# Tiles 2 and 3 join the seven-product scheme in a layer-normed attention and MLP kernel on one core

## The chip, the cores and the metric

The kernel runs on one core of a Trainium2 chip. The time is device microseconds of one launch, as the median of 3 runs. The core has TensorE (PE in the profile; its weight loads are PEld), VectorE (DVE), ScalarE (ACT), GpSimd (POOL) and SyncE (SP), which here only issues transfers. ScalarE issues some transfers too, and waits in its own order to do so.

## The reference, cut to what matters

```python
x = A_x                                    # [1, 2048, 512], float32
xn = layernorm(x)                          # over the last axis, no scale or shift
q, k, v = split(xn @ wqkv)                 # 32 heads of 16
logits = q . k[pos - 2*w], w = 0..7        # times 16 ** -0.5; -1e9 where pos - 2*w < 0
s = (softmax(logits) . v[pos - 2*w]) @ wo
h = relu(xn @ w1 + b1) ** 2                # w1: 512 x 1792
g = silu(h @ w2 + b2)                      # w2: 1792 x 512
out = x + s * g
```

All of it is float32. A product of two float32 matrices is made from three passes: each operand is split into a rounded high part (written by ScalarE) and a low part (the rest, a subtraction on VectorE or GpSimd), and high by high, high by low and low by high are added up in one accumulator.

## The kernel before, in words

The 2048 rows are 16 tiles of 128. The kernel has two stages. In the first, each tile is loaded (`load_x`, line 146), its mean and spread are found (`stats`, `mean`, `spread`), it is normalised (`norm`, line 442), turned so that the 512 columns lie on partitions (`trans`, line 474) and split (`highx`, `lowx`). Tiles 0 to 3 are turned by TensorE (`TURN` is 4). Later tiles are turned in two steps: `shuffle` (line 467) moves blocks by four transfers on SP's queue (`xb<-xn`), and VectorE's stream transpose does the rest. Then q, k and v are formed and stored to DRAM; attention reads them back from there. In the second stage the MLP runs in four chunks of four tiles, and the attention's result meets it through `wo`.

Products of the first stage are made in two ways. The plain way, `qkv(t, s)` (line 526), takes 12 matmuls of 128x512 for one tile and one of q, k, v. The other way, `seven(a)` (line 571), treats a pair of tiles a and a+1 and the q and k columns as a 2 by 2 block product and forms it from seven block products instead of eight, with sums of blocks on both sides. The names: X, Y, Z and U are accumulators; `ss` holds the sums of the pair's turned tiles (four blocks in two buffers: `sum_x` makes the difference `xd` on VectorE and three more sums on GpSimd, `sum_high` and `sum_low` split them, one low part on VectorE and one on GpSimd); T1 to T4 (`t` in the profile) hold the sums of the weight blocks, made once by `sum_w` (line 556): eight subtractions, eight high parts, eight low parts. In the seven way, k's two output tiles are finished by additions on VectorE (`stg<-Z,stg`, `stg<-Y,stg`), while the plain way evacuates each output with one ScalarE copy. v is plain in both ways. Six matmuls make one block product. The last product of a pair, Z with T4, waits in `tail` and is issued in the next pair's turn.

Before the change `SEVEN` is the even tiles 4 to 14: tiles 0 to 3 are plain, and six pairs use seven products.

The order of the instructions on every engine is that of the program's text (`Ordered`, line 75, records each operation, so that all of them have line 87 in the profile). Attention is a generator of pieces of VectorE work of about 2.3 us. `pump(margin)` (line 366) keeps two estimated clocks, one for TensorE and one for VectorE, and lays down pieces as long as VectorE's estimated clock stays below TensorE's plus the margin. Loads of attention's k, q and v (`load`, line 322) are put off to a due time on those clocks and issued on ScalarE's queue.

Of the kernel before, what the change touches and what calls it, by code (L numbers as in the profile page):

```python
# [39 lines left out]

SEVEN = range(4, 15, 2)

# [5 lines left out]
ASIDE = (1, 3, 6, 9, 12)  # L48

STATS = (0, 1, 2, 3, 4, 5, 8, 10, 12)  # L50

MATMUL, TRANSPOSE, DVE_FIXED, SLACK, LATE, ROOM0, ROOM = 227, 150, 170, 500, 3000, 500, 3500

BEHIND, FREE, LAND, LOAD = 5000, 2000, 6000, 11500


@with_exitstack
def body(ctx: ExitStack, tc: tile.TileContext, x, wqkv, wo, w1, b1, w2, b2, out):
# [78 lines left out]
    pss = p1ctx.enter_context(tc.tile_pool(name="pss", bufs=1))  # L137
    G.memset(pxT.tile([P, 24], F32, name="gap"), 0.0)
    xins = {}
# [99 lines left out]
    def attention():  # L239
# [94 lines left out]

# [107 lines left out]
    def norm(t):  # L442
# [31 lines left out]
    def trans(t, aside=False):  # L474
        place(t)
        pTs[t] = piece(f"xs{t}") if t % 2 and t - 1 in SEVEN else psT(f"pxT{t}")
        if t < TURN:
# [19 lines left out]

    sums, ss = {}, {}

    def sum_x(a):  # L500

        xe, t = pTs.pop(a), pTs.pop(a + 1)
        u = piece(f"xd{a}")
        V.tensor_sub(u, xe, t)
# [9 lines left out]

    def sum_high(a):
        ss[a] = [pss.tile([P, 2, 2, 2, P], FR, name=f"ss{a}_{i}", tag="ss", bufs=2) for i in range(2)]
        for t, d in zip(sums[a], ss[a]):
            A.activation(d[:, :, 0], four(t), AF.Copy)

# [35 lines left out]

    def sum_w():
        q, k = raws[0], [raws[1, i] for i in range(KT)]
        for i in range(2):
            V.tensor_sub(q[:, i], k[i], q[:, i])
            V.tensor_sub(k[i], k[2 + i], k[i])  # L560
            V.tensor_sub(k[2 + i], k[2 + i], q[:, i])
            V.tensor_sub(q[:, 2 + i], q[:, 2 + i], k[2 + i])
        for n, src in ((T2, k[2:]), (T1, [q[:, 0], q[:, 1]]), (T3, k[:2]), (T4, [q[:, 2], q[:, 3]])):
            tw[n] = buffer(f"t{n}", n)
            for i in range(2):
                high(tw[n][:, 0, i], None, src[i])
                low(tw[n][:, 0, i], tw[n][:, 1, i], src[i], V)

    tail = []

    def seven(a):
# [28 lines left out]
        if a == SEVEN[0]:  # L600
            sum_high(a)
        first_norm(a)
        second_norm(a)
        pump(LATE)
        qkv(a, 2)
        if a > SEVEN[0]:
            sum_high(a)
        pump(LATE)
        while tail:
            tail.pop()()  # L610
        sum_low(a)
        if more:
            trans(a + 2)
        else:
            load_w(3)
        pump(LATE)
        qkv(b, 2)
        if more:
            trans(b + 2, True)
            lowx(a + 2)  # L620
# [7 lines left out]
        if more:  # L628
            highx(b + 2)
        else:  # L630
# [4 lines left out]
        if more:  # L635
            lowx(b + 2)
            sum_x(a + 2)
            next_stats(a)
        pump(LATE)
        product(Z, s(2), tw[T3])  # L640
        product(Y, s(3), wq[3], stop=True)
        pump(1500)
        V.tensor_add(sk_[:, :, 1], groups(Z), sk_[:, :, 0])
        V.tensor_add(sk_[:, :, 0], groups(Y), sk_[:, :, 0])
        store(a, 1, sk_)
# [7 lines left out]
        if not more:  # L653
# [3 lines left out]
            up(0, 0, psT)  # L657
            tail.pop()()
            next_w()
            pump(1500)  # L660
            up(0, 1, psT)
            lowh(0)
            pump(LATE)
# [88 lines left out]
    qkv(1, 0, lambda: highs(2, 2))  # L752
    trans(3)
    lows(2, 2)
    lowx(3)
    stats(4)
    stats(5)
    next(stream)
# [12 lines left out]
    def first_norm(a):  # L771
        if a + 4 < NT:
            norm(a + 4)

    def second_norm(a):
        if a + 4 < NT:
            norm(a + 5)
# [7 lines left out]

    for a in range(2, NT, 2):
        b = a + 1
        if a >= TPC:
            for t in (a, b):
                dma(sx[t // TPC][:, t % TPC], xt[t].bitcast(F32))  # L790
        if a in SEVEN:
            seven(a)
            if a + 2 < NT:
                pump(LATE)
            if a == 12:
                next_w()
                dma(b1t, b1.rearrange("(f p) -> p f", p=P))
            if a == 10:
                for f in range(3):
                    load_w(f)  # L800
            continue
        qkv(a, 0)
        pump(LATE)
        qkv(b, 0)
        if a == 2:
            first_norm(2)
            second_norm(2)
        trans(a + 2)
        pump(LATE)
        qkv(a, 1)  # L810
        lowx(a + 2)
        trans(b + 2)
        pump(LATE)
        qkv(b, 1)
        lowx(b + 2)
        sum_x(a + 2)
        pump(LATE)
        qkv(a, 2)
        next_stats(a)
        pump(LATE)  # L820
        qkv(b, 2)
        pump(LATE)
    lowh(1)
# [197 lines left out]
```

## Time and profile before

| what | value |
|---|---|
| median of 3 runs | 486.58 us (486.3 to 486.68) |
| the profiled execution, whole | 487.03 us |
| its span, first to last instruction | 485.0 us |
| granted TensorE clock | 0.998 |
| TensorE busy | 478.9 us, 99% of the span |
| VectorE busy | 439.8 us, 91% |
| ScalarE, GpSimd busy | 228.2 us (47%), 173.7 us (36%) |

In the timeline a row gives the start and the length in us, the engine, the line, the operation, what is written from what, the shape and the count, and in brackets how long the engine stood idle just before and what released it. The length of a row of several instructions runs to the end of the last. Neighbouring instructions of one engine overlap a little, so that the step from one start to the next is shorter than the length: matmuls of 128x512 show 389 ns each and follow each other every 227 ns.

### The profile page before, as it was taken

What the parts mean: (1) busy time and instruction counts of PE and PEld (TensorE: products, weight loads), DVE (VectorE), ACT (ScalarE), POOL (GpSimd) and SP (SyncE); (2) the same over time, 40 slices, a digit from 0 to 9 for tenths busy, and PEclk for the clock granted to TensorE, in tenths of its full rate; (3) what the DMA queues carried; (4) which work ended last, traced back from release to release, by engine and by line L of the source; (5) the groups of instructions that cost most, each with busy time, mean ns of one, the idle gap of its engine ahead of it and who ended that gap; (6) DMA issues with size and microseconds to landing.
All of it is one profiled execution on the core that took longest, in us unless ns stands there. A gap on an engine that the chain in (4) does not pass through costs nothing.

```text
span 485.0 us, 5918 instructions
## 1 busy us (share of the span) xinstructions
PE 478.9 (99%) x2118; PEld 394.4 (81%) x2118; DVE 439.8 (91%) x374; ACT 228.2 (47%) x403; POOL 173.7 (36%) x153
## 2 busy tenths in 40 slices
PE   8999999999999999999999999999999999999996
PEld 5888888888788888887888888888888888888885
DVE  5998999999999999999999999999999889999242
ACT  5686667635465774337313533461243365223240
POOL 1326343655798898201233230412032014021100
PEclk9999999999999999999999999999999999999999
DMA  8899898994969782805362428355421846150231
GB/s 280 245 309 314 251 277 282 316 344 174 320 225 298 180 268 92 298 34 190 104 187 64 164 96 283 100 151 166 128 100 67 297 101 170 37 151 0 88 105 68
DMA packets 48520, 88.78 MB, mean 183 GB/s; under 512 B 5372, under 2 KB 32364, under 8 KB 45676
## 3 DMA queue, kind: packets, MB, share of 16 engines
q1 hardware_dynamic: 42444, 51.72, 34.3%
q10 hardware_dynamic: 4320, 33.56, 19.4%
q0 software_dynamic: 1728, 3.15, 4.0%
q8 instruction: 16, 0.26, 0.2%
q14 instruction: 12, 0.10, 0.1%
HBM read 57.94 MB, written 27.32 MB: 176 GB/s over the span
## 4 chain that ended last, share of the span: by engine, by line
PE 98%; DMA 1%; DVE 0%; POOL 0%; issue 0%; ACT 0%; POOLq 0%
PE ph L87 31%; PE pb L87 31%; PE pq L87 14%; PE pw L87 9%; PE Z L87 3%; PE Y L87 3%; PE X L87 3%; PE U L87 2%; DMA x<-in_A_x 1%; PE pxT L87 0%; DVE z L87 0%; DVE st L87 0%; POOL rs L87 0%; DVE xn L87 0%; ACT scratch L87 0%
## 5 line engine op out<-in xcount | busy, mean ns | idle before, releaser
L87 PE MATMUL pb<-w,h 128*128 128x512 f32 x672 | 160.6, 389 | 0.0
L87 PEld LDWEIGHTS pb<-w,h 128*128 128x128 f32 x672 | 126.2, 188 | 26.2
L87 PE MATMUL ph<-xU,w 128*128 128x512 f32 x504 | 120.7, 389 | 0.0
L87 PEld LDWEIGHTS ph<-xU,w 128*128 128x128 f32 x504 | 94.5, 188 | 20.0 <-DVE h L87 0.5
L87 ACT ACTIVATE ph<-ph,b1t 128x512 f32<-128x512 f32 x56 | 36.9, 659 | 145.2 <-PE ph L87 131.6
L87 DVE TENSOR_TENSOR pv<-v,L 128x2048 f32<-128x2048 f32 x32 | 77.8, 2431 | 1.3 <-POOL L L87 0.7
L87 DVE TENSOR_TENSOR pr<-k,q 128x2048 f32<-128x2048 f32 x32 | 78.3, 2447 | 0.6
L87 DVE TENSOR_REDUCE L<-pr 128x128 f32<-128x2048 f32 x32 | 72.9, 2279 | 0.4
L87 DVE TENSOR_REDUCE v<-pv 128x256 f32<-128x2048 f32 x32 | 72.7, 2272 | 0.4
L87 POOL TENSOR_TENSOR h<-sq,h 128x512 fp32r<-128x512 f32 x15 | 25.9, 1729 | 82.1 <-ACT sq L87 79.7
L87 PE MATMUL pw<-wot,oT 128*128 128x512 f32 (+1 forms) x204 | 45.9, 376 | 0.0
L87 DVE TENSOR_TENSOR h<-ph,h 128x512 fp32r<-128x512 f32 x41 | 27.8, 678 | 17.1 <-ACT ph L87 17.1
L87 PEld LDWEIGHTS pw<-wot,oT 128*128 128x128 f32 x204 | 36.8, 188 | 7.1
L87 PE MATMUL ph<-xT,w 128*128 128x512 f32 x168 | 40.2, 389 | 0.0
L87 PEld LDWEIGHTS ph<-xT,w 128*128 128x128 f32 x168 | 31.5, 188 | 6.7 <-DVE h L87 0.2
L87 ACT ACTIVATE h<-ph 128x512 fp32r<-128x512 f32 x56 | 33.5, 599 | 2.5
L87 PE MATMUL pq<-wq,xt 128*128 128x512 f32 x144 | 34.4, 389 | 0.0
L87 POOL TENSOR_TENSOR L<-L,mx_None 128x512 f32<-128x512 f32 x7 | 17.6, 2516 | 41.6 <-DVE mx_None L87 24.2
L87 PEld LDWEIGHTS pq<-wq,xt 128*128 128x128 f32 x144 | 27.0, 188 | 5.6
L87 PE MATMUL pq<-wq,xT 128*128 128x512 f32 x132 | 30.9, 393 | 0.0
L87 PEld LDWEIGHTS pq<-wq,xT 128*128 128x128 f32 x132 | 24.5, 188 | 5.8 <-ACT xT L87 0.7
L87 POOL TENSOR_TENSOR L<-L,sm_None 128x512 f32<-128x512 f32 x7 | 11.4, 1623 | 45.4 <-DVE sm_None L87 45.4
(103 smaller groups left out, 551.4 us busy)
## 6 DMA issues: line engine op xcount, KB each, us to landing
k<-sk ACTq DMA_DIRECT2D x8, 1408.0 KB, 6.4
v<-sv ACTq DMA_DIRECT2D x8, 1408.0 KB, 8.3
sx<-xt SPq DMA_DIRECT2D x12, 512.0 KB, 5.0
xU<-sx ACTq DMA_DIRECT2D x6, 1024.0 KB, 8.8
x<-in_A_x SPq DMA_DIRECT2D x16, 256.0 KB, 5.8
sk<-stg SPq DMA_DIRECT2D x8, 512.0 KB, 4.4
sq<-stg SPq DMA_DIRECT2D x8, 512.0 KB, 4.8
sv<-stg SPq DMA_DIRECT2D x8, 512.0 KB, 5.7
```

The lines of the kernel that those rows point to most:

```text
L87: return tc.keep_in_program_order(f(*a, **k))
```

## The change

`SEVEN` now begins at 2: the pair of tiles 2 and 3 is formed by seven block products too, with tiles that TensorE has turned. The pair's sums need a copy of tile 3's turned tile outside PSUM (`xs`, one more ScalarE copy in `highx`). `sum_w` is cut up: `sub_w` makes six of the eight subtractions before the pair's first product, `last_w` the other two after U; the high and low parts of T1 to T3 are made in `early`, those of T4 in `later`. Statistics of tiles 4 and 5 are put ahead of the second half of v's low weight parts. Tiles 4 and 5 are turned, and tiles 6 and 7 normalised and shuffled, after U of the new pair. The normalisations of tiles 8 to 11 move to other places of their pair (`NORMS`). Attention's first loads get due times of their own (`FIRST`). A pair's evacuation of X stands behind the copy of Z, and the margin of one `pump` in `seven` goes from 1500 to 500.

```diff
-SEVEN = range(4, 15, 2)
+SEVEN = range(2, 15, 2)
+NORMS = {4: "v", 6: "s"}
+FIRST = {"k": 10000, "q": 10000, "v": 16000}
...
-                defer(max(clock["V"] + FREE if u else 0, done_tiles[n][1][u] + LAND), start)
+                defer(max(clock["V"] + FREE if u else 0, done_tiles[n][1][u] + (LAND if u else FIRST[n])), start)
...
     def highx(t):
         A.activation(xt[t][:, 0], pTs[t].rearrange("p (k n) -> p k n", k=KT), AF.Copy)
+        if t == TURN - 1:
+            sums[t] = spare(f"xs{t}", t - 1)
+            A.activation(sums[t], pTs[t], AF.Copy)
...
-    def sum_w():
+    def sub_w(i, steps=range(3)):
         q, k = raws[0], [raws[1, i] for i in range(KT)]
+        for n in steps:
+            to, a, b = ((q[:, i], k[i], q[:, i]), (k[i], k[2 + i], k[i]), (k[2 + i], k[2 + i], q[:, i]))[n]
+            V.tensor_sub(to, a, b)
...
+    def last_w():
+        for a, b in zip(tparts[T4], tparts[T2]):
+            V.tensor_sub(a, a, b)
...
         if a == SEVEN[0]:
-            sum_high(a)
-        first_norm(a)
-        second_norm(a)
+            early()
+        norms(a, "X")
...
         product(X, x(a, 1), wq[1], stop=True)
-        A.activation(sq_[:, :, 0], groups(X), AF.Copy, scale=0.25)
         pump(LATE)
         product(Y, s(1), tw[T2])
         Z = psH(f"Z{a}")
         A.activation(Z, Y, AF.Copy)
+        if a == SEVEN[1]:
+            highx(a + 2)
+            lowx(a + 2)
+        A.activation(sq_[:, :, 0], groups(X), AF.Copy, scale=0.25)
...
-        pump(1500)
+        pump(500)
         V.tensor_add(sk_[:, :, 1], groups(Z), sk_[:, :, 0])
+        if a == SEVEN[0]:
+            low_w(T4, V)
...
     trans(3)
-    lows(2, 2)
-    lowx(3)
     stats(4)
     stats(5)
+    lows(2, 2)
+    lowx(3)
+    sum_x(2)
     next(stream)
     qkv(0, 2)
     norm(4)
     norm(5)
     shuffle(4)
-    pump(LATE)
-    mean(6)
+    sub_w(0)
+    sub_w(1)
+    for t in (6, 7):
+        mean(t)
+        spread(t)
     qkv(1, 2)
-    spread(6)
-    mean(7)
-    spread(7)
-    sum_w()
-    pump(LATE)
+    pump(-9000)
+
+    def early():
+        flush(clock["PE"])
+        for n in (T2, T1, T3):
+            high_w(n, (0,))
+        sum_high(2, (0,))
+        high_w(T2, (1,))
+        sum_high(2, (1,))
+        for n in (T1, T3):
+            high_w(n, (1,))
+        low_w(T2, V, (0,))
+        sum_low(2)
+        low_w(T2, V, (1,))
+        low_w(T1, V)
+        low_w(T3, V)
+        pump(LATE)
+
+    def later():
+        trans(4)
+        trans(5, True)
+        last_w()
+        lowx(4)
+        highx(5)
+        norm(6)
+        norm(7)
+        shuffle(6)
+        pump(LATE)
+        high_w(T4)
+        lowx(5)
+        sum_x(4)
...
-    for a in range(2, NT, 2):
-        b = a + 1
+    for a in SEVEN:
...
-        qkv(a, 0)
-        pump(LATE)
-        qkv(b, 0)
...
-        qkv(b, 2)
-        pump(LATE)
+        seven(a)
+        if a + 2 < NT:
+            pump(LATE) if a > SEVEN[0] else after()
```

Three places show how the order moves. The first is VectorE while TensorE forms v of tile 0. In the rows, `wq_121` is the half of v's split weights that v's second six matmuls read, `xT` the turned first tiles, `st`, `mv`, `rs` the statistics of tiles 4 and 5. Before:

```order
L87 TENSOR_TENSOR xT_168<-pxT_285,xT_168 128x512
L87 TENSOR_TENSOR wq_121<-wqraw_141,wq_121 128x512 x2
L87 TENSOR_TENSOR xT_168<-pxT_315,xT_168 128x512
L87 BN_STATS st_324<-x_166 128x6
L87 BN_AGGR mv_326<-st_324 128x2
L87 TENSOR_SCALAR rs_327<-mv_326 128x1
L87 BN_STATS st_331<-x_188 128x6
```

And with the change:

```order
L90 TENSOR_TENSOR xT_168<-pxT_285,xT_168 128x512
L90 BN_STATS st_323<-x_166 128x6
L90 BN_AGGR mv_325<-st_323 128x2
L90 TENSOR_SCALAR rs_326<-mv_325 128x1
L90 BN_STATS st_330<-x_188 128x6
L90 BN_AGGR mv_332<-st_330 128x2
L90 TENSOR_SCALAR rs_333<-mv_332 128x1
L90 TENSOR_TENSOR wq_121<-wqraw_141,wq_121 128x512 x2
L90 TENSOR_TENSOR xT_168<-pxT_315,xT_168 128x512
L90 TENSOR_TENSOR xd_340<-pxT_285,xs_321 128x512
```

Six statistics instructions now stand ahead of the two low weight parts, and the difference `xd` of tiles 2 and 3 is new behind them.

The second place is GpSimd at the same time, with the scale factors `rs` of tiles 4 to 7 and the sums `xs`, `xd` of a pair. Before:

```order
L87 TENSOR_TENSOR rs_334<-rs_334,mhalf 128x1
L87 TENSOR_SCALAR rs_385<-rs_385 128x1
L87 TENSOR_TENSOR rs_385<-rs_385,mhalf 128x1
L87 TENSOR_TENSOR shift_386<-mean_367,rs_385 128x1
L87 TENSOR_SCALAR rs_395<-rs_395 128x1
L87 TENSOR_TENSOR rs_395<-rs_395,mhalf 128x1
L87 TENSOR_TENSOR shift_396<-mean_392,rs_395 128x1
L87 TENSOR_TENSOR xs_496<-xs_496 128x256
```

And with the change:

```order
L90 TENSOR_TENSOR rs_333<-rs_333,mhalf 128x1
L90 TENSOR_TENSOR xs_321<-xs_321 128x256
L90 TENSOR_TENSOR xs_321<-xs_321,xd_340 128x256
L90 TENSOR_TENSOR xd_340<-xd_340 128x256
L90 TENSOR_SCALAR rs_381<-rs_381 128x1
L90 TENSOR_TENSOR rs_381<-rs_381,mhalf 128x1
L90 TENSOR_TENSOR shift_382<-mean_378,rs_381 128x1
L90 TENSOR_SCALAR rs_391<-rs_391 128x1
L90 TENSOR_TENSOR rs_391<-rs_391,mhalf 128x1
L90 TENSOR_TENSOR shift_392<-mean_388,rs_391 128x1
L90 TENSOR_TENSOR ss_1_435<-xd_340,ss_1_435 128x2x256
L90 TENSOR_TENSOR xs_508<-xs_508 128x256
```

Three sums and one low part (`ss_1`) for the pair of tiles 2 and 3 are new. The first three depend on `xd` of VectorE, behind which VectorE's order has the normalisations of tiles 4 and 5 and six subtractions of weight blocks; the fourth depends on ScalarE's high part, at a place where VectorE's order has low parts of T1 to T3.

The third place is VectorE behind the difference `xd` of tiles 4 and 5, whose arrival starts three sums on GpSimd. Before:

```order
L87 TENSOR_TENSOR xd_517<-pxT_476,xs_496 128x512
L87 BN_STATS st_537<-x_355 128x6
L87 BN_AGGR mv_539<-st_537 128x2
L87 TENSOR_SCALAR rs_540<-mv_539 128x1
L87 TENSOR_TENSOR pr_0_602<-k_365,q_430 128x2048
```

And with the change:

```order
L90 TENSOR_TENSOR xd_530<-pxT_504,xs_508 128x512
L90 TENSOR_TENSOR stg_1_418<-Z_492,stg_1_418 128x4x128
L90 TENSOR_TENSOR t_526<-wqraw_134,t_526 128x512 x2
L90 TENSOR_TENSOR stg_1_418<-Y_426,stg_1_418 128x4x128
L90 BN_STATS st_552<-x_362 128x6
L90 BN_AGGR mv_554<-st_552 128x2
L90 TENSOR_SCALAR rs_555<-mv_554 128x1
L90 TENSOR_TENSOR pr_0_572<-k_413,q_463 128x2048
```

Two additions that finish k of tiles 2 and 3 are new there, and T4's two low parts (`t`) now stand between them.

More of the change, by code (lines that the diff above doesn't have):

```diff
@@ L137, in body @@
     pss = p1ctx.enter_context(tc.tile_pool(name="pss", bufs=1))
-    G.memset(pxT.tile([P, 24], F32, name="gap"), 0.0)
+    G.memset(pxT.tile([P, 104], F32, name="gap"), 0.0)
     xins = {}
@@ L459, in norm @@
             load_x(t + 4)
+    sums, ss = {}, {}
     def place(t):
@@ L475, in trans @@
         place(t)
-        pTs[t] = piece(f"xs{t}") if t % 2 and t - 1 in SEVEN else psT(f"pxT{t}")
+        pTs[t] = piece(f"xs{t}") if t % 2 and t > TURN else psT(f"pxT{t}")
         if t < TURN:
@@ L496, in lowx, with spare @@
             pTs.pop(t)
-    sums, ss = {}, {}
+    def spare(name, a):
+        return att.tile([P, 512], F32, name=name, tag="L", bufs=2) if a == SEVEN[0] else piece(name)
     def sum_x(a):
         xe, t = pTs.pop(a), pTs.pop(a + 1)
-        u = piece(f"xd{a}")
+        t = sums.pop(a + 1, t)
+        u = spare(f"xd{a}", a)
         V.tensor_sub(u, xe, t)
@@ L513, in four, with sum_high @@
         return ap.rearrange("p (s k n) -> p s k n", s=2, n=P)
[L515 to L518, printed above, removed]
+    def sum_high(a, parts=(0, 1)):
+        if 0 in parts:
+            ss[a] = [pss.tile([P, 2, 2, 2, P], FR, name=f"ss{a}_{i}", tag="ss", bufs=2) for i in range(2)]
+        for i in parts:
+            A.activation(ss[a][i][:, :, 0], four(sums[a][i]), AF.Copy)
     def sum_low(a):
@@ L554, in body, with high_w, low_w @@
     tw = {}
[L556 removed]
+    tparts = {}
+    def sub_w(i, steps=range(3)):
         q, k = raws[0], [raws[1, i] for i in range(KT)]
[L558 to L563, printed above, removed]
[L564 to L567 removed]
+        for n in steps:
+            to, a, b = ((q[:, i], k[i], q[:, i]), (k[i], k[2 + i], k[i]), (k[2 + i], k[2 + i], q[:, i]))[n]
+            V.tensor_sub(to, a, b)
+        tparts.update({T2: k[2:], T1: [q[:, 0], q[:, 1]], T3: k[:2], T4: [q[:, 2], q[:, 3]]})
+    def last_w():
+        for a, b in zip(tparts[T4], tparts[T2]):
+            V.tensor_sub(a, a, b)
+    def high_w(n, parts=(0, 1)):
+        if 0 in parts:
+            tw[n] = buffer(f"t{n}", n)
+        for i in parts:
+            high(tw[n][:, 0, i], None, tparts[n][i])
+    def low_w(n, eng, parts=(0, 1)):
+        for i in parts:
+            low(tw[n][:, 0, i], tw[n][:, 1, i], tparts[n][i], eng)
     tail = []
@@ L607, in seven @@
             sum_high(a)
+        norms(a, "s")
         pump(LATE)
@@ L610, in seven @@
             tail.pop()()
[L611 to L614, printed above, removed]
+        now = SEVEN[0] < a and more
+        if a > SEVEN[0]:
+            sum_low(a)
+        if now:
+            trans(a + 2, a == SEVEN[1])
+        if not more:
             load_w(3)
@@ L617, in seven @@
         qkv(b, 2)
-        if more:
+        if now:
             trans(b + 2, True)
-            lowx(a + 2)
+            if a > SEVEN[1]:
+                lowx(a + 2)
+        norms(a, "v")
         pump(LATE)
         product(X, x(a, 1), wq[1], stop=True)
-        A.activation(sq_[:, :, 0], groups(X), AF.Copy, scale=0.25)
         pump(LATE)
@@ L627, in seven @@
         A.activation(Z, Y, AF.Copy)
-        if more:
+        if a == SEVEN[1]:
+            highx(a + 2)
+            lowx(a + 2)
+        A.activation(sq_[:, :, 0], groups(X), AF.Copy, scale=0.25)
+        if now:
             highx(b + 2)
-        else:
+        if not more:
             next_w()
@@ L634, in seven @@
         A.activation(sk_[:, :, 0], groups(U), AF.Copy)
-        if more:
+        norms(a, "U")
+        if now:
             lowx(b + 2)
@@ L638, in seven @@
             next_stats(a)
+        if a == SEVEN[0]:
+            later()
         pump(LATE)
```

61 lines of the change are left out of this document (22 added, 39 removed).

## The prediction

> **What bounds the kernel now.** First the page's busy times and its chain of waits:
>
> ```profile
> PE 478.9 (99%) x2118; PEld 394.4 (81%) x2118; DVE 439.8 (91%) x374; ACT 228.2 (47%) x403; POOL 173.7 (36%) x153
> PE 98%; DMA 1%; DVE 0%; POOL 0%; issue 0%; ACT 0%; POOLq 0%
> ```
>
> TensorE sets the end, so a matmul less is time less, as long as TensorE finds its operands ready. Whether it does is read from the stage that changes. TensorE's timeline there:
>
> ```profile
> 19.96 22.04 PE L87 MATMUL pq<-wq,xT 128*128 128x512 f32 x96
> 50.00 1.52 PE L87 MATMUL Y<-t,ss 128*128 128x512 f32 x6
> 51.36 1.52 PE L87 MATMUL U<-t,ss 128*128 128x512 f32 x6
> 55.44 1.52 PE L87 MATMUL X<-wq,xt 128*128 128x512 f32 x6
> 124.81 1.68 PE L87 MATMUL Y<-t,ss 128*128 128x512 f32 x6
> 133.33 1.67 PE L87 MATMUL Z<-t,xt 128*128 128x512 f32 x6
> ```
>
> Six matmuls step by 51.36 - 50.00 = 1.36 us, 0.227 each. There is no gap until the last pair's Y, which takes 1.68 instead of 1.52: here TensorE waits 0.16 us, at Z 0.15 us. So VectorE is just in time there. Its busy time, and what it waited for, from the first place where its order changes (19.44) to the end of the last pair's sums (`ss`, 125.24):
>
> ```profile
> 19.44:125.24 105.80, 105.80 (x470) 87.41 (x468) 98.66 (x115) 62.95 (x123) 49.04 (x61) 1.00 0.88 277
> ...
> DVE xt L87 <- ACT xt L87: 2.9, 4, 0.9
> DVE ss L87 <- ACT ss L87: 1.1, 2, 0.6
> DVE pxT L87 <- DMA xb<-xn: 0.9, 1, 0.9
> DVE xn L87 <- POOL rs L87: 0.4, 1, 0.4
> DVE xT L87 <- ACT xT L87: 0.2, 1, 0.2
> ```
>
> The third busy time of the first row is VectorE's: 98.66 of 105.80 us. The waits, in the second view, add up to 5.5 us; the rest is steps between dependent instructions. In this stage VectorE has 5.5 us to give and no more, and TensorE has no slack against it at the end of the stage.
>
> **What is removed.** q and k of tiles 2 and 3 take 48 matmuls before (four times 12) and 42 after (seven products of 6): -6 x 0.227 = -1.36 us. TensorE's waits of 0.16 and 0.15 belong to the stage and are made anew below.
>
> **Statistics ahead of v's weights.** VectorE's rows, before:
>
> ```profile
> 19.44 1.28 DVE L87 TENSOR_TENSOR wq<-wqraw,wq 128x512 fp32r<-128x512 f32 x2
> 20.93 0.69 DVE L87 TENSOR_TENSOR xT<-pxT,xT 128x512 fp32r<-128x512 f32 x1 [0.21 <-ACT xT L87]
> 21.54 0.68 DVE L87 BATCH_NORM_STATS2 st<-x 128x6 f32<-128x512 f32 x1
> 22.54 0.68 DVE L87 BATCH_NORM_STATS2 st<-x 128x6 f32<-128x512 f32 x1
> 23.55 0.54 DVE L87 TENSOR_SCALAR xn<-x,mv,rs 128x512 f32<-128x512 f32 x1
> ```
>
> Statistics of a tile step by 1.00 us. With two tiles' ahead, the first low part ends at 19.44 + 2.00 + 0.69 = 22.13. TensorE's v of tile 0 starts at 19.96; its eighth matmul, the first that reads that part, is due at 19.96 + 7 x 0.227 = 21.55. It waits about 0.6 us. The second part (22.73) is needed three matmuls later, about 22.9, and costs nothing. What this delay hides behind: nothing, TensorE has no other work in its order. It only matters, though, if VectorE is not later still at the end of the stage.
>
> **VectorE's account to the last pair.** The same pieces of attention stand ahead of the last pair's sums before and after, so the account is what is added, less the waits that close up. Added are four instructions: `xd`, `ss` low, and the two additions that finish k. Their steps are in these rows:
>
> ```profile
> 57.23 0.68 DVE L87 TENSOR_TENSOR stg<-Z,stg 128x512 f32<-128x512 f32 x1
> 58.02 0.69 DVE L87 TENSOR_TENSOR stg<-Y,stg 128x512 f32<-128x512 f32 x1
> 58.63 0.41 DVE L87 TENSOR_TENSOR L<-L,mask 128x256 f32<-128x256 f32 x1
> 62.08 0.68 DVE L87 TENSOR_TENSOR ss<-xs,ss 128x512 fp32r<-128x512 f32 x1
> 62.68 0.72 DVE L87 STREAM_TRANSPOSE pxT<-xb 128x512 f32<-128x512 f32 x1
> ```
>
> 0.79 + 0.61 + 0.60, and for `xd`, of the same size, 0.60 once more: 2.6 us. The eight weight subtractions and eight low parts are only moved. On GpSimd the pair adds three sums and a low part, off the path by themselves (GpSimd is busy 49.04 of the 105.80 us). But GpSimd and VectorE stop each other. The rows that show it, VectorE's and GpSimd's:
>
> ```profile
> 88.78 2.28 DVE L87 TENSOR_TENSOR pv<-v,L 128x2048 f32<-128x2048 f32 x1
> 107.29 1.78 DVE L87 TENSOR_TENSOR ss<-xs,ss 128x512 fp32r<-128x512 f32 x1
> 120.40 3.13 DVE L87 TENSOR_TENSOR pr<-k,q 128x2048 f32<-128x2048 f32 x1
> 123.46 1.78 DVE L87 TENSOR_TENSOR ss<-xs,ss 128x512 fp32r<-128x512 f32 x1
> ...
> 54.26 0.74 POOL L87 TENSOR_TENSOR xs<-xs 128x256 f32<-128x256 f32 x1 [5.49 <-ACT scratch L87]
> 62.41 1.50 POOL L87 TENSOR_TENSOR ss<-xd,ss 128x512 fp32r<-128x512 f32 x1 [3.32 <-ACT ss L87]
> 88.95 2.17 POOL L87 TENSOR_SCALAR rs<-rs 128x1 f32<-128x1 f32 x1
> 106.33 2.19 POOL L87 TENSOR_TENSOR ss<-xd,ss 128x512 fp32r<-128x512 f32 x1 [2.77 <-ACT ss L87]
> 120.10 1.29 POOL L87 TENSOR_TENSOR w<-w2r,w 128x512 fp32r<-128x512 f32 x1
> 121.35 3.34 POOL L87 TENSOR_TENSOR ss<-xd,ss 128x512 fp32r<-128x512 f32 x1
> ```
>
> A one-column operation on GpSimd (88.95) takes 2.17 us and ends with VectorE's 2.28 us product. VectorE's `ss` takes 0.68 us alone (62.08), 1.78 where GpSimd's `ss` holds until 108.52 (107.29) and again until 124.69 (123.46): GpSimd had waited for the product ahead, went first, and VectorE waited 1.1 us. The product of 120.40 lost 0.85 us to GpSimd's 1.29. So where both engines have such work, they take turns, and each turn costs VectorE up to GpSimd's length.
>
> After the change GpSimd's three sums (0.74 each, 2.2 us) are released by `xd` just as VectorE has normalisations and six weight subtractions one after the other, all from SBUF; its low part (1.3 to 1.5) falls among T1 to T3's low parts; and the sums of tiles 4 and 5, which before met statistics, now meet T4's two low parts (2 x 0.74). Bounds for what VectorE loses: nothing (GpSimd might always wait, as at 88.95), or 2.2 + 1.4 + 1.5 = 5.1 us. Where GpSimd's instruction was already waiting it went first each time above, so I take the new pair's in full and the meeting with T4 half: 2.2 + 1.3 + 0.7 = 4.2 us.
>
> Of the 5.5 us of waits some remain. ScalarE still has to hand over tile 4's high part, and the shuffle's transfer and the sums' high parts can still be late; with VectorE itself later, most are over before it asks. Bounds 0 and 5.5; I take 0.9, one wait of the largest kind in the list.
>
> The sum: VectorE ends the last sums at 125.24 + 2.6 + 4.2 - (5.5 - 0.9) = 127.44 us. TensorE's third matmul of that Y, which reads them, would be due without any wait at 124.81 + 0.45 - 1.36 = 123.90, and with 0.18 us for the handing over (124.81 + 0.45 + 0.16 - 125.24 before) it starts at 127.62. TensorE has then waited 3.7 us in the stage, the 0.6 from above among them; wherever in the stage these lie, they add up to this. Against before: -1.36 + 3.72 - 0.16 = +2.2, less the 0.15 at Z, which now stands twelve matmuls further back: **about +2.0 us**. Behind this TensorE runs without gaps, so it reaches the end whole: 487.03 + 2.0 for the profiled execution, which lies 0.45 above the median, so **488.6 us** as a median.
>
> **Edits at nothing.** The moved normalisations of tiles 8 to 11, the evacuation of X behind Z's copy, and attention's later first loads lie on ScalarE (62.95 of 105.80 us busy) and in transfers that are asked for later; without that cover each would cost a ScalarE step of 0.5 us. The margin of 500 for 1500 lays a 2.2 us piece of attention behind k's additions instead of ahead of them: it moves where TensorE waits (later pairs, rather than the additions), not the account, since the piece stands ahead of the last sums either way.
>
> **A rule beside it.** The Trainium skill, in "SBUF — State Buffer", section "Who interferes with whom", says that a VectorE instruction with two SBUF inputs excludes a GpSimd instruction that reads SBUF for its whole length and the other way round, and that `tensor_scalar` in its two-port mode does too. The first half is what the rows show. The second half no row here shows: the two normalisations of tiles 4 and 5, with one SBUF input, would lose one sum's 0.74 us as well. By that rule, the estimate would go up by no more than this, to about 489.3.
>
> **The rivals.** *VectorE catches up, faster.* If GpSimd always waits (0 lost) and the waits close up, VectorE is ready at 125.24 + 2.6 - 4.6 = 123.24, ahead of TensorE. Then only v's 0.6 stands against the gain: -1.36 + 0.6 - 0.3 = -1.1, 485.5 us. For it: VectorE's work of one product always held GpSimd back when it came first. Against: all of 107.29, 120.40, 123.46. 13%.
>
> *A draw.* GpSimd goes first in half the meetings (2.1 us lost): 2.0 - 2.1 = -0.1, 486.5 us. For it: the pair's sums are released when VectorE has just begun an instruction, and GpSimd lies idle half of the time. 25%.
>
> *Behind before by more: the shuffle of tiles 6 and 7.* It now stands behind tile 4's store and two loads on SP's queue, and behind two normalisations on ScalarE. Before, VectorE waited for it:
>
> ```profile
> 36.72 2.55 SPq L472 DMA_DIRECT2D xb<-xn  x4
> 38.48 0.52 ACTq L87 DMA_DIRECT2D v<-sv  x1
> 34.56 1.51 ACT L87 ACTIVATE xn<-x,shift,rs 128x512 f32<-128x512 f32 x2
> 47.45 0.73 DVE L87 STREAM_TRANSPOSE pxT<-xb 128x512 f32<-128x512 f32 x1 [0.90 <-DMA xb<-xn]
> ```
>
> U of the new pair ends near 36.9 (72 matmuls behind 19.96, and the 0.6); then come three copies and the two normalisations, 3 us, so the shuffle is issued near 40, 3 us later. After the transposes (1.7) come two pieces of attention (4.5) and the low part (0.7), 6.9 us, ahead of X of that pair, whose third matmul is due at 55.44 + 0.45 - 1.36 = 54.5. Landing later than 47.6 decides; at 47.45 + 3 = 50.4 VectorE stands idle for about 2 us more, and the time is 490.6. Against: the wait before was behind attention's big load of v, which is issued later now. 12%.
>
> **How the numbers follow.** The forecast has 50% and is 488.6. To tell a change, 0.2% is needed, 0.97 us: faster is below 485.6, slower above 487.55. Faster holds the first rival, 13%; same the draw, 25%; slower the forecast and the shuffle, 62%. The range leaves out about half of the first rival and of the last: 485.6 to 490.4; the forecast's own, with 3.2 to 5.1 us lost to GpSimd, is 487.6 to 489.5.
>
> **What would show it.** Right: v of tile 0 with a gap of about 0.6 us near 21.6; GpSimd's first three sums of length 0.7 to 1.4 with VectorE's normalisation or subtractions at 1.2 to 1.5 us instead of 0.54 and 0.69; VectorE without waits of half a microsecond from 25 to 125 but for one or two; TensorE's waits at Y of pairs 6, 12 or 14, near 66, 112 and 128 us, 3 to 4 us in all. Wrong: VectorE's subtractions at 0.69 throughout, or a TensorE that reaches the last Y within 0.3 us of its due time, or waits of TensorE in the second stage that were not there before.

## The result

| | before | changed kernel |
|---|---|---|
| median | 486.58 us (486.30 to 486.94) | 495.06 us (494.87 to 496.59) |
| span of the profiled execution | 485.0 us | 493.0 us |
| its granted clock, mean | 0.998 | 0.995 |

The ratio is 1.0183, 95% interval 1.0167 to 1.0200: 8.5 us slower, where 2.0 were forecast. One thing is needed to read the runs further down: in some profiled executions, one of the kernel before with a small addition among them, TensorE's first six products take 4.7 us instead of 2.8 and all that follows comes 1.9 us later, so where a median lies oddly the profiled execution's own gaps say more.

### The profile page after: what moved, and what is told of

Its sections match the earlier page's. It is cut to its first block, busy times and chain, and to the rows that moved or that the text cites. A ratio compares the mean times of both kernels' runs of the same rounds, so it can differ in the third digit from the quotient of the medians.

```text
span 493.0 us, 5919 instructions
## 1 busy us (share of the span) xinstructions
PE 481.9 (98%) x2112; PEld 394.1 (80%) x2112; DVE 445.5 (90%) x378; ACT 229.2 (47%) x407; POOL 182.8 (37%) x157
## 4 chain that ended last, share of the span: by engine, by line
PE 80%; DVE 9%; DMA 6%; POOL 2%; issue 1%; ACT 1%; SPq 0%; DVEq 0%; POOLq 0%
PE ph L90 31%; PE pb L90 31%; PE pw L90 9%; PE pq L90 4%; DMA xb<-xn 3%; DMA v<-sv 2%; DVE pr L90 2%; PE Y L90 2%; PE Z L90 2%; DVE L L90 1%; PE U L90 1%; DVE wq L90 1%; DVE ss L90 1%; POOL rs L90 1%; PE X L90 1%
## 5 line engine op out<-in xcount | busy, mean ns | idle before, releaser
L90 DVE TENSOR_TENSOR pv<-v,L 128x2048 f32<-128x2048 f32 x32 | 79.0, 2469 | 1.3 <-POOL L L90 0.7
L90 DVE TENSOR_TENSOR pr<-k,q 128x2048 f32<-128x2048 f32 x32 | 76.9, 2404 | 0.6
L90 PE MATMUL pq<-wq,xt 128*128 128x512 f32 x144 | 36.0, 401 | 0.0
L90 PEld LDWEIGHTS pq<-wq,xt 128*128 128x128 f32 x144 | 28.2, 196 | 6.1
L90 POOL TENSOR_TENSOR w<-w2r,w 128x512 fp32r<-128x512 f32 x14 | 32.4, 2312 | 0.1
L90 POOL TENSOR_TENSOR L<-L,mx_None 128x512 f32<-128x512 f32 x7 | 15.6, 2222 | 41.6 <-DVE mx_None L90 24.2
L90 POOL TENSOR_TENSOR xs<-xs 128x256 f32<-128x256 f32 x7 | 11.1, 1580 | 43.4 <-DVE xd L90 34.7
```

Of the source, the lines that this page charges most:

```text
L90: return tc.keep_in_program_order(f(*a, **k))
```

## The profile after

The page's busy times and chain of waits, changed kernel:

```profile
PE 481.9 (98%) x2112; PEld 394.1 (80%) x2112; DVE 445.5 (90%) x378; ACT 229.2 (47%) x407; POOL 182.8 (37%) x157
PE 80%; DVE 9%; DMA 6%; POOL 2%; issue 1%; ACT 1%; SPq 0%; DVEq 0%; POOLq 0%
```

The six matmuls are gone (2112 for 2118), but TensorE's share of the chain has fallen from 98% to 80%, and TensorE is busy 3 us longer with fewer matmuls. Its timeline in the first stage tells where:

```profile
19.97 1.86 PE L90 MATMUL pq<-wq,xT 128*128 128x512 f32 x7
22.22 4.14 PE L90 MATMUL pq<-wq,xT 128*128 128x512 f32 x17 [0.39 <-DVE wq L90]
...
38.44 1.52 PE L90 MATMUL Y<-wq,ss 128*128 128x512 f32 x6
41.17 0.73 PE L90 MATMUL X<-wq,xt 128*128 128x512 f32 x2 [1.22 <-ACT xt L90]
43.22 1.40 PE L90 MATMUL X<-wq,xt 128*128 128x512 f32 x4 [1.31 <-DVE xt L90]
44.41 4.32 PE L90 MATMUL pq<-wq,xt 128*128 128x512 f32 x12
48.57 1.52 PE L90 MATMUL Z<-t,xT 128*128 128x512 f32 x6
...
100.19 1.99 PE L90 MATMUL Y<-t,ss 128*128 128x512 f32 x6 [0.28 <-ACT ss L90]
117.49 1.20 PE L90 MATMUL Y<-t,ss 128*128 128x512 f32 x4 [0.81 <-DVE ss L90]
133.67 1.21 PE L90 MATMUL Y<-t,ss 128*128 128x512 f32 x4 [0.90 <-DVE ss L90]
```

Read from start to start, with 0.227 us for each matmul: X of the pair of tiles 4 and 5 should begin at 39.80 and has lost 1.4 us when it begins, and 1.9 more before the v products of 44.41. These twelve then step to 48.57 in 4.16 us instead of 2.72, another 1.4: a matmul takes up to twice as long. That is the clock, in the windows view (the granted TensorE clock is the number ahead of the last two; it is 1.00 in the first stretch, in which TensorE pauses, and 0.51 in the second):

```profile
40.00:44.00 4.00, 1.52 (x5) 0.97 (x6) 4.00 (x7) 3.11 (x6) 0.00 (x0) 1.00 0.03 12
44.00:47.00 3.00, 3.00 (x9) 2.29 (x8) 3.00 (x5) 2.00 (x6) 2.42 (x3) 0.51 0.98 281
```

The same sum for every place, with three of the runs that follow (us lost against 0.227 for each matmul; small gaps count with the place ahead of them):

| place | before | changed | early k | norms behind | lows held |
|---|---|---|---|---|---|
| v of tile 0 | 0 | 0.8 | 0.8 | 0.8 | 0.8 |
| X of tiles 4, 5, and the clock behind it | 0.1 | 4.7 | 0 | 0 | 0 |
| Y of tiles 6 | 0 | 0.9 | 1.1 | 1.0 | 1.2 |
| Y of tiles 10 | 0 | 1.3 | 1.3 | 0 | 0 |
| Y of tiles 12 | 0 | 1.1 | 1.1 | 0.4 | 0 |
| Y of tiles 14 | 0.2 | 1.2 | 1.2 | 1.2 | 0 |
| first stage, with all small gaps | 0.35 | 10.11 | 5.77 | 3.62 | 2.02 |
| second stage | 0.68 | 0.28 | 1.49 | 0.07 | 0.40 |
| span | 485.0 | 493.0 | 489.9 | 486.3 | 484.9 |

The tally closes: 485.0 - 1.36 + (10.11 - 0.35) + (0.28 - 0.68) = 493.0, and in the same way 489.9, 486.3 and 485.0 for the other three, to 0.1 us. All of it is of single profiled executions. The dip of the clock is not in every execution: 3 us at 0.51 take 0.003 off the mean, and one with a mean of 0.999 took 495.05 us, as much as those with 0.995 to 0.997.

VectorE's waits in the stage (us in total, times, the longest), changed kernel:

```profile
DVE pxT L90 <- DMA xb<-xn: 4.8, 2, 4.1
DVE ss L90 <- ACT ss L90: 2.6, 1, 2.6
DVE xt L90 <- ACT xt L90: 0.6, 1, 0.6
```

and the two long ones in its timeline:

```profile
31.52 4.18 DVE L90 TENSOR_TENSOR t<-wqraw,t 128x512 fp32r<-128x512 f32 x5
39.76 0.73 DVE L90 STREAM_TRANSPOSE pxT<-xb 128x512 f32<-128x512 f32 x1 [4.06 <-DMA xb<-xn]
...
100.24 0.69 DVE L90 TENSOR_TENSOR ss<-xs,ss 128x512 fp32r<-128x512 f32 x1 [2.63 <-ACT ss L90]
```

VectorE stands idle from 35.7 to 39.76 for the shuffle of tiles 4 and 5, and for 2.63 us for the sums of tiles 10 and 11. Two questions for the runs: who made each of these late, and what does the time become without them.

## The experiments

**The early k.** SP issues the shuffle at 25.75 to 28.35 in the changed kernel and at 25.52 to 28.47 before, so it is not asked for later. What differs is attention's first load of k on ScalarE's queue: issued at 23.09 before, at 26.65 now, amid the shuffle. The transfer view of the changed kernel from 27 to 38 us (queue q10 is ScalarE's, with k and q in it, q1 SP's; packets, MB, share of the 16 engines' time):

```profile
q10 hardware_dynamic: 282, 1.95, 56.9%
q1 hardware_dynamic: 1380, 1.40, 42.9%
```

k and q take more than half of the engines' time, in packets of 6.9 KB on average against 1.0 KB. The Trainium skill says in "DMA: Bandwidth & Descriptors", section "Queues, rings and completion order", that an engine serves its queues in turn and a whole packet of each; the shares are sums over 11 us, and no run here shows the turns themselves.

```diff
+START = {"k": 0, "q": 10000, "v": 16000}
...
+                defer(max(clock["V"] + FREE if u else 0, done_tiles[n][1][u] + (LAND if u else START[n])), start)
...
     shuffle(4)
+    flush(clock["PE"])
     sub_w(0)
```

> Edit: the changed kernel, with only the transfer of attention's first k issued about 3 us earlier (ahead of the means of tiles 6 and 7 on ScalarE, near 24 us instead of 27.3); every other instruction keeps its place. Theory A (the first loads crowd the shuffle of tiles 4 and 5, and VectorE's account decides behind that): the shuffle lands near 35 instead of 39.57, VectorE's wait of 4.06 us for it and TensorE's 3.2 us of waiting at X of tiles 4 and 5 go, and with them the dip of the granted clock (0.72 from 43 to 49 us, 1.44 us of time). Not all of the 4.7 us comes back, because VectorE has gained only its 4.06: about 491.0 us, with TensorE's waits at the Y of later pairs a little larger than in the changed kernel. Rival B (the shuffle is late for its own sake, by its place on SP's queue): landing stays near 39.5 and the time at 495. Rival C (only TensorE's chain counts): all 4.7 us come back, 490.3 or less, and the later waits keep their size.

Measured: 490.79 us (489.91 to 491.74), ratio 1.0076 (1.0049 to 1.0104). VectorE, then TensorE, at the place:

```profile
36.05 0.73 DVE L91 STREAM_TRANSPOSE pxT<-xb 128x512 f32<-128x512 f32 x1 [0.24 <-DMA xb<-xn]
...
39.95 1.52 PE L91 MATMUL X<-wq,xt 128*128 128x512 f32 x6
41.31 2.88 PE L91 MATMUL pq<-wq,xt 128*128 128x512 f32 x12
44.03 1.52 PE L91 MATMUL Z<-t,xT 128*128 128x512 f32 x6
```

k is issued at 23.88 here. Half of the result, 4.3 us, is the place of one transfer on another queue. The time is theory A's, and so is the path. VectorE's order is the same, instruction for instruction; its wait for the shuffle is 3.8 us shorter, and a softmax subtraction beside GpSimd's low part takes 0.94 us (at 61.76) instead of 1.46 (at 65.56), so that the last sums start 4.27 us earlier (127.58 for 131.85). The last Y goes on 4.27 us earlier too, at 129.40. TensorE itself was rid of 4.7 us at X of tiles 4 and 5, pauses and half clock together: what it gained beyond VectorE it lost again at Y of tiles 6.

**k and q behind the shuffle.** The loads of k and q are held back and issued together, by `release`, at 33.42 and 34.09.

```diff
+        release()
         A.activation(Z, Y, AF.Copy)
```

> Edit: the changed kernel, with the transfers of attention's first k and first q issued only behind k's and q's last evacuations ahead of Z's copy on ScalarE (near 34 us), so that the shuffle of tiles 4 and 5 has the queues to itself; every other instruction keeps its place. Theory A: the shuffle lands near 32 to 33, 6 us earlier; VectorE and TensorE no longer wait there; k and q land near 41 to 42, ahead of their first use (48.5 in the changed kernel, near 45 if the 4 us are gained). About 491.0 us as with the early k, or up to 1 us less. Rival B (its own queue): shuffle still near 39, 495. Rival D (k and q now crowd what follows, the loads of tiles 10 and 11 and the next shuffle): the first wait goes, a new one of 2 us or more comes near 45 to 50, 493 or more.

Measured: 492.29 us (490.92 to 493.68), ratio 1.0105 (1.0068 to 1.0142). Again no wait at the first shuffle; but the second one now meets the tail of the loads:

```profile
35.77 0.71 DVE L90 STREAM_TRANSPOSE pxT<-xb 128x512 f32<-128x512 f32 x1
49.12 0.73 DVE L90 STREAM_TRANSPOSE pxT<-xb 128x512 f32<-128x512 f32 x1 [1.68 <-DMA xb<-xn]
```

So the crowding is shown from both sides: move the loads either way and the first wait goes; move them later and the next shuffle pays (theory A, with some of rival D). How the two queues share the transfer engines is not shown by this.

**The statistics, undone.**

```diff
-    stats(4)
-    stats(5)
     lows(2, 2)
     lowx(3)
+    stats(4)
+    stats(5)
```

> Edit: the changed kernel, with the low parts of v's weights and of tile 3 ahead of the statistics of tiles 4 and 5 on VectorE, as before the change. (The planner lays some later pieces of attention on other sides of k's additions.) Theory A: v of tile 0 loses its gap of 0.66 us, and X of tiles 4 and 5 waits 0.66 us longer, since the landing of the shuffle at 39.57 sets it; the time stays at 495 within 0.4. Rival: the gap is a loss of its own, and the time falls by 0.7 to 494.4.

Measured: 493.21 us, but from 491.94 to 496.34, ratio 1.0133 (1.0085 to 1.0182): this run decides nothing about the gap. The two executions at 492 had a granted clock of 1.000, the others 0.993 (494.12) and 0.991 (496.34, the profiled one). What it shows is the clock: in the profiled execution TensorE paused 2.43 and 1.06 us at X of tiles 4 and 5, and ran at half clock for six:

```profile
42.00:48.00 6.00, 4.94 (x12) 3.42 (x12) 6.00 (x10) 4.51 (x9) 2.84 (x3) 0.51 0.55 170
```

**T4 on GpSimd.** If VectorE's account decides, taking four instructions off it must show.

```diff
-            V.tensor_sub(a, a, b)
+            G.tensor_sub(a, a, b)
...
-            low_w(T4, V)
...
+        low_w(T4, G)
```

> Edit: as with the early k, and besides T4's two subtractions and two low parts on GpSimd instead of VectorE (GpSimd is idle from 33.4 to 44.5 us); attention's pieces keep their place. VectorE has 2.6 us less to do ahead of the last pair (4 instructions of 0.60 to 0.69), up to 3.3 with what GpSimd's sums cost it there. Theory A (behind the shuffle VectorE's account decides): 2.5 to 3.3 us less than the early k alone, about 488.2 us. Rival C (TensorE's chain alone): within 0.5 us of the early k. Rival E (the turns of GpSimd and VectorE eat it): VectorE's transposes and low parts near 40 to 47 at 1.2 us or more, and a gain under 1 us.

Measured: 492.02 us (491.44 to 493.13), ratio 1.0104 (1.0064 to 1.0143): no gain over the early k. VectorE's low parts of T1 to T3, first with the early k and then in this run, with GpSimd's subtractions for T4 beside them:

```profile
31.62 4.18 DVE L91 TENSOR_TENSOR t<-wqraw,t 128x512 fp32r<-128x512 f32 x5
...
31.41 6.38 DVE L91 TENSOR_TENSOR t<-wqraw,t 128x512 fp32r<-128x512 f32 x5
33.21 3.43 POOL L91 TENSOR_TENSOR wqraw<-wqraw,wqraw 128x512 f32<-128x512 f32 x2
```

and VectorE later in this run:

```profile
44.66 2.81 DVE L91 TENSOR_TENSOR pr<-k,q 128x2048 f32<-128x2048 f32 x1 [0.88 <-POOL t L91]
48.77 0.69 DVE L91 TENSOR_TENSOR ss<-xs,ss 128x512 fp32r<-128x512 f32 x1 [1.30 <-ACT ss L91]
...
97.28 0.69 DVE L91 TENSOR_TENSOR ss<-xs,ss 128x512 fp32r<-128x512 f32 x1 [2.63 <-ACT ss L91]
```

GpSimd's turns took more than the 2.6 us of work that was moved: 2.2 us at the low parts, 0.88 ahead of the product and half a us within it, and 1.30 for sums that GpSimd made later. VectorE starts the product ahead of the sums of tiles 10 and 11 at 92.36, and with the early k at 91.04, so it is 1.3 us later, not earlier, and so is the last Y (130.72 for 129.40). That is rival E, and more than it said; this run never gave VectorE the time that theory A was to be tested with. The wait of 2.63 us at the sums of tiles 10 and 11 came along with VectorE, unchanged in length. It needs a cause.

**What the sums of tiles 10 and 11 wait for.** With the early k, GpSimd, ScalarE and VectorE there are, in the changed kernel 4.3 us later, alike:

```profile
91.07 2.67 POOL L91 TENSOR_TENSOR rs<-rs,mhalf 128x1 f32<-128x1 f32 x1
...
94.04 0.82 ACT L91 ACTIVATE xn<-x,shift,rs 128x512 f32<-128x512 f32 x1 [2.48 <-POOL shift L91]
94.76 0.58 ACT L91 ACTIVATE stg<-pq 128x512 f32<-128x512 f32 x1
95.24 0.62 ACT L91 ACTIVATE ss<-xs 128x512 fp32r<-128x512 f32 x1
...
91.04 2.29 DVE L91 TENSOR_TENSOR pv<-v,L 128x2048 f32<-128x2048 f32 x1
95.96 0.69 DVE L91 TENSOR_TENSOR ss<-xs,ss 128x512 fp32r<-128x512 f32 x1 [2.63 <-ACT ss L91]
```

A one-column operation on GpSimd (0.55 us elsewhere) starts 0.03 us behind VectorE's product and takes 2.67; ScalarE stands for it with a normalisation that is needed only for the transposes at 113.08, and v's evacuation and the sums stand behind ScalarE; then VectorE waits for the sums. The product that begins this comes from VectorE itself.

```diff
-NORMS = {4: "v", 6: "s"}
+NORMS = {4: "v", 6: "s", 10: "s"}
```

> Edit: as with the early k, and the normalisations of tiles 14 and 15 stand behind the high parts of the sums of tiles 10 and 11 on ScalarE, instead of ahead of v's evacuation; VectorE's, GpSimd's and TensorE's orders are the same. Theory F (the chain GpSimd, ScalarE, VectorE): with the early k a small step of tile 15's spread on GpSimd takes 2.67 us beside VectorE's product at 91.04, ScalarE stands 2.48 us for it with v's evacuation and the sums behind it, VectorE then 2.63 us, and TensorE pays at Y of tiles 10, 12 and 14 (0.95, 1.09 and 1.20). With the edit the sums' high parts end near 93.0 instead of 96.4, VectorE's wait of 2.63 goes, and of TensorE's 3.2 us in these three places about 0.6 is left: 2.6 less, near 488.2. Theory A' (VectorE has more work than time from the first pair on, so waits only move): less than 1 us. Rival G: the shuffle of tiles 14 and 15, issued later, is late: VectorE waits for it near 110, and nothing is gained.

Measured: 488.33 us (487.81 to 489.85, 10 executions), ratio 1.0028 (1.0014 to 1.0043), 2.5 us below the early k (2.3 by the ratios, each to the kernel before as measured beside it). VectorE and the last Y:

```profile
93.29 0.68 DVE L91 TENSOR_TENSOR ss<-xs,ss 128x512 fp32r<-128x512 f32 x1
...
127.22 1.20 PE L91 MATMUL Y<-t,ss 128*128 128x512 f32 x4 [0.89 <-DVE ss L91]
```

The wait is gone, TensorE's loss at Y of tiles 10 with it, and 0.7 of 1.1 at Y of tiles 12. At Y of tiles 14 nothing was gained: 0.6 us in all were to be left in these three places, 1.6 are. VectorE's last sums and the last Y come 2.18 us earlier. That the time was right to 0.2 us is in part luck: of the profiled execution's gain, 1.4 us are waits of the early k's execution in the second stage (1.49 in the table), of which the expectation says nothing. The chain of theory F is shown, at about 2.2 us.

**The margin.**

```diff
-        pump(500)
+        pump(1500)
```

> Edit: as with the early k, and the margin of attention's pieces ahead of k's additions is 1500 again, as before the change. One piece each in the pairs 6 and 8 changes sides with k's two additions. Theory (this edit moves where TensorE waits, not how much): within 0.5 us of the early k, 490.8. Rival: a product instead of a reduction beside GpSimd's sums and spreads makes ScalarE's or VectorE's wait of 2.6 us near 93 go or double: 2 us or more to one side.

Measured: 490.93 us (490.64 to 491.48), ratio 1.0072 (1.0047 to 1.0098), 0.1 from the early k, whose other edits it shares. Nothing, as expected.

**What is left: VectorE's time.** On the run with the norms behind, both low parts of the last two pairs go to VectorE, and in a second run the low parts of v's weights go first too (the edit of the undone statistics); the planner may put pieces of attention elsewhere for it:

```diff
-        for t, d, eng in zip(sums.pop(a), ss[a], (V, G)):
+        for t, d, eng in zip(sums.pop(a), ss[a], (V, G if a < 12 else V)):
```

> Edit: the one before, and for the pairs 12 and 14 both low parts of the sums on VectorE instead of one on GpSimd. (Two pieces of attention and k's additions change sides in these pairs.) Theory: VectorE's low part there takes 1.78 us beside GpSimd's, and two low parts of its own take 1.3, so 0.5 us is gained in each pair: the wait at Y of tiles 14 goes, near 487.6. Rival: VectorE is the bound all the same, and TensorE's waits in these pairs are within 0.3 of the run before.

> Edit: the one before, and the low parts of v's weights and of tile 3 ahead of the statistics of tiles 4 and 5 as before the change. Theory: TensorE's 0.66 us at v of tile 0 goes and is not made up for, now that no landing behind it decides: 0.6 less, near 487.0, the kernel before within 0.2%. Rival: it comes back as a longer wait at Y of tiles 6, which is 1.1 us with the early k: no gain.

Measured: 489.57 us (486.60 to 491.69), ratio 1.0038 (1.0012 to 1.0064), and 489.18 (488.15 to 491.42), ratio 1.0046 (1.0028 to 1.0065). Both drop TensorE's losses at Y of tiles 10 to 14 to nothing and gain nothing: waits come up in the second stage, 2.8 and 3.8 us there by the gaps. The row for it, of the second run:

```profile
PE ph L91 <- DVE h L91: 1.2, 4, 0.4
```

The planner's other places for pieces of attention are one reason that VectorE's low parts of `h` could be late. ScalarE and VectorE show another one in that run:

```profile
162.94 0.63 ACT L91 ACTIVATE w<-w2r 128x512 fp32r<-128x512 f32 x1 [7.43 <-DMA w2r<-in_B_w]
...
165.27 0.69 DVE L91 TENSOR_TENSOR h<-ph,h 128x512 fp32r<-128x512 f32 x1 [3.93 <-ACT ph L91]
```

ScalarE stands 7.4 us for a block of the MLP's weights, the parts of `h` stand behind that in its order, and VectorE idles 3.9 us for them. From 134 to 235 us VectorE waits 4.0 and 5.0 us in this way in these two runs; 1.9 with the early k, whose pieces keep their place and which loses 1.5 us in the second stage; 0.2 to 0.3 in the changed kernel and with the norms behind, which lose 0.3 and 0.1 there. So the pieces are not shown to be the cause. Why the weights land late in one run and not in another stays open.

The same two again, with all pieces held at their place, by taking back from VectorE's estimated clock what the edits add to it (703 for each low part, 600 for the other order):

> Edit: early k, tile 14's and 15's normalisations behind the sums, and both low parts of the last two pairs' sums on VectorE, with all of attention's pieces held at their place (in the run with two low parts the planner had put some of them later). Theory H (VectorE's time is what counts from 44 us on, and a piece put later is paid later): VectorE saves 0.5 us in each of the two pairs and puts nothing off, so TensorE's waits at Y of tiles 12 and 14 (0.41 and 1.18) shrink by about 1.0 and no new waits come in the second stage: 487.3. Rival: TensorE's waits come back in the second stage, ahead of the up and down products near 170 to 225, as in the run with two low parts: 488.3 or more.

> Edit: the one before, and the low parts of v's weights and of tile 3 ahead of the statistics of tiles 4 and 5, with all of attention's pieces held at their place. VectorE's work is the same. Theory H: TensorE's 0.8 us at v of tile 0 goes, but VectorE is not earlier for it, so the wait comes back at Y of tiles 6 or later: within 0.3 us of the run before. Rival (the gap is a loss of its own): 0.7 less, 486.6.

Measured: 488.34 us (486.36 to 490.22), ratio 1.0029 (1.0009 to 1.0048), and 488.41 (487.00 to 488.68), ratio 1.0028 (1.0016 to 1.0040). Of the first, the profiled execution (486.71) loses 2.0 us in the first stage, 1.6 less than with the norms behind, and 0.4 in the second, as theory H has it. By the median it gained nothing: four of its ten executions lie from 486.4 to 487.0, the traced one among them, and six from 488.2 to 490.2, and what the six lost is not shown. The second answers what the undone statistics could not: TensorE's 0.8 us at v goes, and X of tiles 4 loses 0.4 and X of tiles 6 0.7 instead, so that the first stage loses no less than before. In the traced executions the gap is no loss of its own. The 1.8 us in the second stage of this run come with 1.5 us of VectorE's waiting behind ScalarE and the weights, as above.

The bare price of VectorE's work, in the kernel before:

```diff
-        V.tensor_sub(u, xe, t)
+        for n in range(5 if a == SEVEN[0] else 1):
+            V.tensor_sub(u, xe, t)
...
```

> Edit: the kernel before the change, with the difference xd of tiles 4 and 5 made five times instead of once (the same result; four more instructions on VectorE, 0.60 each, 2.4 us, near 47 us); everything else keeps its place. This measures the bare price of the four instructions that the change adds to VectorE. By the account of the prediction (waits ahead of the last pair close up): VectorE's waits behind this place are 0.64, 0.56 and 0.58, so 2.4 - 1.8 = 0.6 us is left at the last pair: 487.2. Theory H with no slack in the second stage either: up to 2.4 us, 489.0. Rival (VectorE's slack takes all): within 0.2 of before.

Measured: 490.70 us (488.61 to 491.01), ratio 1.0070 (1.0045 to 1.0094). The profiled execution (490.68) has the slow first products, 1.9 us, which the sums do not touch; by its gaps TensorE loses 2.7 us in the first stage instead of 0.35, so 2.4 us of VectorE cost 2.3. Not at the last pair: at the next link,

```profile
56.25 1.65 PE L87 MATMUL Z<-t,ss 128*128 128x512 f32 x6 [1.38 <-ACT Z L87]
```

where ScalarE's copy Z stands behind sums and normalisations that GpSimd, started later, hands over later. The waits that the expectation let close up did not: VectorE's list there still has 3.1 and 1.2 us. One of the four executions stands apart, at 488.61, 2.0 above the kernel before.

**The second shuffle first.** On the lows held, one more place on SP's queue:

```diff
         shuffle(6)
+        load_x(10)
+        load_x(11)
```

(and these two loads no longer in the normalisations ahead of it.)

> Edit: as with the lows held, and on SP's queue the shuffle of tiles 6 and 7 stands ahead of the loads of tiles 10 and 11; nothing else moves. With the lows held VectorE waits 1.00 us for this shuffle (transposes at 48.12) and TensorE loses 1.2 us at Y of tiles 6, near 65; the profile has 2.0 us of TensorE's waits from v of tile 0 on (0.8 there and 1.2 here), against 0.65 before the change. Theory H: the shuffle is issued 1.2 us earlier and lands near 47, VectorE has 1.0 us more, and TensorE's waits at Y of tiles 6 fall to 0.2: 1.0 us less than the lows held, 0.7 us below the kernel before in like executions (486.0), which is within 0.2%. Rival (transfers share what there is): the shuffle still lands near 48, and nothing changes.

Measured: 487.02 us (486.18 to 491.02, 13 executions), ratio 0.9997 (0.9981 to 1.0013). VectorE's wait for that shuffle is 0.2 us and TensorE's loss at Y of tiles 6 0.9 instead of 1.2; the second stage has a wait of 0.94 instead, and about 2 us more in all than with the lows held, in an execution that is the slowest of the thirteen (491.02) and in which VectorE waits 1.8 us behind ScalarE and the weights. So the change with all this mended stands where the kernel before stands. A version that beats both was not found.

## Why the prediction was wrong

The direction was right and the size was not: +8.5 us for +2.0. The path was right as well: VectorE's account to the last sums sets the time. The step that failed is a term of that account, the waits. Step by step:

- **What is removed**, 1.36 us: right, the tally closes with it.
- **Statistics ahead of v's weights**, about 0.6: right (0.66), and so was the reservation that it matters only if VectorE is not later still: with it undone the waits came back at X of tiles 4 and 6. The medians, 488.41 against 488.34, could not tell 0.6 us, since one of the runs spreads over 3.9.
- **VectorE's account**, its busy part, 2.6 us of instructions and 4.2 to GpSimd: about right. Its busy time in the stage (the third busy time of the row in the windows view):

```profile
19.44:133.60 114.16, 108.86 (x464) 86.68 (x462) 104.64 (x119) 64.00 (x126) 56.94 (x66) 0.99 0.80 257
```

and the groups that grew:

```profile
L90 DVE TENSOR_TENSOR t<-wqraw,t 128x512 fp32r<-128x512 f32 x8 | 6.9, 912 | 0.0
L90 DVE TENSOR_TENSOR wqraw<-wqraw,wqraw 128x512 f32<-128x512 f32 x8 | 6.3, 802 | 0.1
L90 DVE TENSOR_TENSOR L<-L,mx 128x256 f32<-128x256 f32 x2 | 1.9, 940 | 0.1
```

  104.64 less 98.66 is 6.0, for 6.8. By the mean lengths GpSimd's turns cost 1.8 at the low parts of T1 to T4 (912 ns for 681), 0.9 at the subtractions (802 for 690), 0.4 at the normalisations, and 1.0 at a place that was not listed, a softmax subtraction beside GpSimd's low part (940 for 424): 4.1, part of which overlaps with a neighbour. The two terms were sized about right, by places that were not all the right ones.
- **The waits, the step that failed**: "Bounds 0 and 5.5; I take 0.9". They are 8.0, above both bounds. The last sums end at 133.6, which is 127.44 with 7.1 more for waits and 0.8 less for work, to 0.1 us. The bounds let old waits close up and did not let new ones arise. The two that arose, 4.06 and 2.63, have their causes in what the prediction had at nothing or not at all: a load of k laid on the shuffle, and a step of GpSimd that holds ScalarE and, behind it, the sums.
- **"Edits at nothing"**: attention's later first loads were put there because they are "transfers that are asked for later". The load of k was 3.6 us later, which laid it on the shuffle; 4.3 us by experiment. The half clock that followed cost TensorE 1.4 us on the spot, but the last Y stands 0.9 us for VectorE with it and without it; that the clock is part of the 4.3 is not shown. The margin was rightly at nothing (0.1 us). The evacuation of X behind Z's copy was not tried.
- **"Wherever in the stage these lie, they add up"** held. In every run in which TensorE still waits at the last Y, that Y goes on 1.82 us behind the start of VectorE's last sums, however TensorE's losses ahead of it lie (us):

| run | last sums of VectorE start | last Y goes on |
|---|---|---|
| changed | 131.85 | 133.67 |
| statistics undone | 132.27 | 134.09 |
| k and q behind | 129.14 | 130.96 |
| T4 on GpSimd | 128.90 | 130.72 |
| margin | 128.05 | 129.87 |
| early k | 127.58 | 129.40 |
| norms behind | 125.40 | 127.22 |

  What the account lacked is that the change makes waits where there were none. The cause of the second one, GpSimd's small step beside VectorE's product, was a row of the prediction itself (88.95, 2.17 us); what was not followed is who stands behind GpSimd: ScalarE, and the sums in ScalarE's order.
- **The rival of the second shuffle** did not come in: VectorE waited 0.7 us for it, 0.9 before, and 2 more were named. GpSimd winning or losing half of its turns (the draw, and the rival in which VectorE catches up) was not what decided.
- With both waits taken out the kernel stands at 488.33, where 488.6 was forecast, and the last Y goes on at 127.22, for 127.62. TensorE then loses 3.6 us in the stage, for 3.7. VectorE still waits 1.9 us there, for the 0.9 taken, so part of that agreement is luck.

What was to be seen, was: the gap near 21.6 and waits at Y of tiles 6, 12 and 14 of 3.2 us. GpSimd's first three sums took 0.8 to 1.2 us, with VectorE's normalisations and subtractions at up to 0.96 and 1.23. "VectorE without waits of half a microsecond from 25 to 125" is what failed.

## What to carry to other kernels

A load that is made later is not free because nobody waits for it: look what it then shares the transfer engines with, above all small packets that somebody does wait for. A sum over an engine's work needs the waits that the change can make, not only those that it finds: before adding up, follow each instruction that another engine can hold to the end of the queue behind it, over all engines. Moving work off a full engine helps only if the engine that takes it does not stop the full one for as long: T4 on GpSimd cost VectorE more than it saved. And where the engine off the path is nearly as full as the one on it (VectorE 90% here), a change that gives TensorE 1.4 us and adds 2.6 to VectorE may have no gain to find; no order tried here found one.

## What the runs showed of the hardware

- Two pauses of TensorE of 1.2 and 1.3 us, with two matmuls between them, were followed by 3 us at a granted clock of 0.51; single pauses of 0.8 to 0.9 us (117.49, 133.67) by none, nor a single one of 1.38 us in the kernel before with four more instructions (56.25; clock 1.00 from 54 to 60 us). The Trainium skill, in "TensorE: Matmul & The Clock Gate", section "What's actually happening", puts the drop behind an idle window of about 3.4 us; in the changed kernel no pause was half as long, so the measurement decides: two short ones close together were enough there.
- The first six products are slow though the granted clock of the records is 1.00 there, and not always equally slow. The timeline of the kernel before (0.45 us from one to the next on average, for 0.227 later):

```profile
6.75 2.84 PE L87 MATMUL pq<-wqraw,scratch 128*128 128x512 f32 x6 [0.16 <-ACT scratch L87]
```

and of the kernel before with four more instructions (0.77 us):

```profile
6.90 4.77 PE L87 MATMUL pq<-wqraw,scratch 128*128 128x512 f32 x6
```

  What makes the difference is not shown.
